# Conversion pieces, weight splits and second-layer weight sums placed anew over the blocks of the expert sweeps, and the last output tile stored in halves

## The chip, the cores and the metric

The kernel runs on one core of a Trainium2 chip. Five engines with instruction queues of their own work side by side: PE (TensorE, matmuls and their weight loads), DVE (VectorE), ACT (ScalarE), POOL (GpSimd) and SP (SyncE, which here only issues DMAs). The metric is the device time of one execution in microseconds (us), lower is better.

## The reference

Three layers follow each other on 2304 tokens of width 512 (4 batches of 576, 8 heads of 64):

```
scores = scale * q k^T;  ret = scores * Dmat (decay, lower triangle);  x = ret v
logits = x @ w_gate;  noisy = logits + log1p(exp(x @ w_noise)) * noise
top2 of 8 experts per token, softmax weights over the two
out[token] += weight * (relu(x @ w1[e]) @ w2[e])     # E=8, 512 -> 1024 -> 512
h = out @ w_in;  g = h * clip(h + 3, 0, 6) / 6;  y = g @ w_out   # 512 -> 2048 -> 512, w_in and w_out in float64
```

## The kernel before, in words

**Order of the work.** The program order of every engine is the order in which the code emits it: nothing is moved later. Each engine takes its instructions in that order, and SP takes its DMA issues in that order, so an instruction that waits holds up all that stand behind it on its engine.

**Precision.** Matmuls take a value as two parts, a rounded high part (written by ACT) and the remainder (written by DVE), and multiply three of the four pairs. So each weight has to be split: `w_load` (L557, L559) loads one quarter of an expert as two tiles of 512 KB, `w_split` (L567) sets up the four tiles for the parts, and `wstep` (L590 on ACT, L591 on DVE) does a quarter of that split at a time. Sixteen such steps belong to one expert.

**Sweeps and blocks.** `moe` (L778 on) goes through ten sweeps `si`. Sweep 0 takes the first 360 tokens of expert 0, sweep 1 its other 256; sweeps 2 to 7 take experts 1 to 6 with both runs of tokens together (360 and 256); sweeps 8 and 9 take expert 7 in two parts. Each sweep has eight blocks `f`, one for each 128 hidden units. In a block, PE first does the first product of each run (`g1`, L737, into the PSUM tiles `ga` and `gb`); ACT then writes the high part of the hidden values (L795), DVE the remainder (L796), and that frees the PSUM tile for the next first product into it. Then PE does the second product of the block before (`flush`, `g2`, L754). In sweep 1 a block has a single run, and `ga` and `gb` take turns.

**Work fitted between.** Beside this a block carries, in this order: up to two weight steps; one DMA load of a token tile for the next sweep (`x_load`, four issues at L682); one tile turned and split (`x_tile`: DVE transpose L690, ACT L692, and at the end of the block the DVE remainder L693); conversion pieces; and one step of `pr_step`.

**Conversion pieces.** The float64 weights of the last layer are turned into float32 in 64 pieces of 128 x 256: `cv_load` (SP, L614, 256 KB), `cv_abs` (ACT, L621), `cv_run` (DVE L632, L633, L635, L637; ACT L639; POOL L640, L641) and `cv_store` (SP, L648; the newest piece is always kept back). `CV` says how many pieces a block of sweeps 2 on runs: before, 2, 2, 2, 1, 1, 1, 1, 1. In a block of these sweeps the order is run, load, store, abs for each piece, so a piece is loaded ahead of its use. In sweep 1 before, blocks 5 to 7 load a piece each and block 7 does one abs.

**Sums.** `pr_step` (L1021 to L1031) makes sums and differences of the converted `w_in`, splits them and stores them to DRAM (`wc`), in seven jobs for each of eight column groups.

**The end.** `o_out` (L1221 on) copies the last four output tiles out of PSUM and stores them: the first three copies on ACT, the last on DVE; the first store from SP, the other three from ACT.

Of the kernel before, what the change touches and what calls it, by code (L numbers as in the profile page):

```python
# [12 lines left out]
AF = mybir.ActivationFunctionType  # L13
# [13 lines left out]
WN, WM = 2, 0  # L27
GA = 14
HS = np.array([0, 1, 3, 2, 4, 5, 7, 6])
CV = (2, 2, 2, 1, 1, 1, 1, 1)  # L30
MORE = -(-(N - CAP) // 128)
REG = CAP + 2048
assert MORE * 128 <= 2048
P = 128
# [44 lines left out]
class K:  # L79
# [686 lines left out]
    def moe(self, xs0):  # L766
        nc = self.nc
        xs = {(0, 0): xs0}
        self.prev = None
        for si, sw in enumerate(self.SW):  # L770
            nxt = self.SW[si + 1] if si + 1 < len(self.SW) else []
            todo = [(e, r, j) for e, r in nxt for j in range((3, 2)[r])]
            get = list(todo)
            e = sw[0][0]
            accs = None
            for f in range(8):
                n = e * 4 + f // 2
                cur = e * 4 if si in (0, len(self.SW) - 2) else n  # L778
                if f % 2 == 0:
                    if si == 0 or self.wsp <= cur + (4, 3, 3, 3, 3, 3, 3, 3, 5, 6)[si]:  # L780
                        self.w_split()
                if f % 2 == 0 and (si, f) != (0, 6) or (si, f) == (0, 7):
                    self.w_load()
                self.wstep(0, n)
                if (si, f) == (0, 7):
                    for s in todo:
                        self.x_fin(*s)
                tf = 3 if si == 1 or len(todo) > 3 else 4
                w, fi = self.w[n], f % 2
                subs = []  # L790
                for q, (_, r) in enumerate(sw):
                    c = (NA, NB)[r]
                    hh, hl = self.hid([P, c]), self.hid([P, c])
                    p = self.g1(self.parts(w, fi), xs[sw[q]], c, "ga" if (r == 0) == (f % 2 == 0 or len(sw) == 2) else "gb")
                    nc.scalar.activation(hh, p, AF.Relu)  # L795
                    nc.vector.scalar_tensor_tensor(hl, p, 0.0, hh.bitcast(F32), op0=OP.max, op1=OP.subtract)  # L796
                    subs.append((hh, hl, (RA, RB)[r]))
                if si == 0:
                    self.rstep()
                    self.send()  # L800
                    if f == 7:
                        for s in todo:
                            self.x_tile(s[0], xs[s[:2]], s[2], "acc", s[1])
                self.wstep()
                self.flush()
                later = []
                self.wstep(later=later if si == 1 else None)
                if accs is None:
                    accs = [[self.pacc([P, DM]) for _ in range(self.run_of(*s)[1])] for s in sw]
                self.prev = [(w, fi, [(*s, a) for s, a in zip(subs, accs)], f == 0, f == 7)]  # L810
                self.fin = (self.y_out, sw, accs)

                if si == 0:
                    for _ in range(3):
                        self.rstep()
                        self.send()
                    if f == 4:
                        while self.sent < NT or self.live:
                            self.rstep()
                            self.send()  # L820
                        self.count()
                        self.slots_in()
                g = 4 if si == 0 else 0
                if f == g:
                    for s in nxt:
                        if si == 0:
                            self.x_load(*s)
                        xs[s] = self.x_new(s[1])
                    if si < 2:
                        self.fill(range(2, E) if si else range(1, 2))  # L830
                if si and get:
                    ee, rr, j = get.pop(0)
                    self.x_load(ee, rr, [j])
                sub = None
                if si and f >= tf and todo:
                    ee, rr, j = todo.pop(0)
                    sub = self.x_tile(ee, xs[ee, rr], j, r=rr)
                if si > 1:
                    for _ in range(CV[f]):
                        self.cv_run()  # L840
                        self.cv_load()
                        self.cv_store()
                        self.cv_abs()
                elif si and f > 4:
                    self.cv_load()
                    if f == 7:
                        self.cv_abs()
                for s in later:
                    s()
                if sub:  # L850
                    sub()
                if (si > 2 or si == 2 and f > 3) and not (si in (6, 7) and f == 7):
                    self.pr_step()
                if si == 7 and f in (0, 2):
                    self.pr_step()
                if si == len(self.SW) - 1:
                    self.x2_prep(0, f - 1)
                    if f in (5, 7):
                        self.wc_load(f // 7)
            for s in sw:  # L860
                xs.pop(s)
# [358 lines left out]
    def o_out(self, t0, acc):  # L1220
        nc = self.nc  # L1221
        for j, a in enumerate(acc):
            o = self.row([P, DM])
            last = t0 + len(acc) == NT

            if last and j == len(acc) - 1:
                nc.vector.tensor_copy(o, a)
            else:
                nc.scalar.activation(o, a, AF.Copy)
            q = nc.scalar if last and j else nc.sync  # L1230
            q.dma_start(self.out[(t0 + j) * P:(t0 + j + 1) * P, :], o)


# [205 lines left out]
```

## Time and profile before

| | us |
|---|---|
| median of 3 runs | 935.1 (935.05 to 935.69) |
| the profiled execution, device time | 936.64 |
| its span, first to last instruction | 934.5 |
| PE busy in the span | 921.8 (99%) |
| DVE busy | 606.8 (65%) |
| ACT busy | 466.5 (50%) |
| POOL busy | 235.9 (25%) |

The device time of the profiled execution is 2.1 us over its span. Busy times of PE are modelled for pipelined matmuls. A timeline row gives the start, the time taken, the engine, the line, the operation, the tiles, and in square brackets how long the engine stood idle before it and for whom. PEld is PE's weight load, which runs ahead of the matmul that uses it. A row of an engine with "q" (SPq, ACTq) is a DMA issue.

### The profile page before, as it was taken

How to read it: one execution, taken by the hardware profiler on the slowest of the kernel's cores; microseconds unless marked ns; L12 is line 12 of the kernel's file. 1: busy time of each engine (PE TensorE's matmuls, PEld its weight loads, DVE VectorE, ACT ScalarE, POOL GpSimd, SP SyncE). 2: the span in 40 equal slices, each digit the busy share in tenths (PEclk: the TensorE clock that was granted, in tenths of full speed). 3: DMA queues.
4: the chain of work that ended last, by engine and by line, in shares of the span. 5: the costliest groups of instructions: out<-in, count | busy, mean ns of one | idle time of the engine just before them, and what ended most of it. 6: DMA issues, size and time to landing. Idle time of an engine off the chain costs nothing.

```text
span 934.5 us, 17789 instructions
## 1 busy us (share of the span) xinstructions
PE 921.8 (99%) x6314; PEld 818.2 (88%) x6314; DVE 606.8 (65%) x1327; ACT 466.5 (50%) x1025; POOL 235.9 (25%) x324
## 2 busy tenths in 40 slices
PE   9999999999999999999999999999999999999996
PEld 6887888988988889888888899999889998999985
DVE  5787747878879797787847446545745554564442
ACT  4666435455564645545544445544554464455432
POOL 1345531324233242432400221042004113300000
PEclk9999999999999999999999999999999999999999
DMA  9964877859879688896636787877578676846541
GB/s 339 386 243 147 304 243 232 238 187 280 259 241 282 227 256 271 248 267 218 224 111 214 265 298 252 307 247 240 188 262 270 205 258 227 271 166 228 167 150 49
DMA packets 123742, 221.22 MB, mean 237 GB/s; under 512 B 13037, under 2 KB 60915, under 8 KB 123643
## 3 DMA queue, kind: packets, MB, share of 16 engines
q1 hardware_dynamic: 113819, 190.47, 61.9%
q0 software_dynamic: 9392, 28.73, 9.1%
q8 instruction: 52, 0.85, 0.4%
q10 hardware_dynamic: 432, 0.79, 0.2%
q14 instruction: 47, 0.39, 0.1%
HBM read 163.97 MB, written 55.97 MB: 235 GB/s over the span
## 4 chain that ended last, share of the span: by engine, by line
PE 86%; DVE 7%; DMA 3%; issue 1%; ACT 1%; POOL 1%; SPq 0%; DVEq 0%; ACTq 0%; POOLq 0%
PE p L754 39%; PE ga L737 12%; PE gb L737 9%; PE mga L1168 7%; PE p L1168 5%; PE mgb L1168 2%; PE mtp L1168 2%; PE sc L225 2%; DVE b L591 1%; PE px L249 1%; PE p L293 1%; DVE cvt L635 1%; PE p L209 1%; DMA xe<-s,free 1%; DVE h L796 1%
## 5 line engine op out<-in xcount | busy, mean ns | idle before, releaser
L754 PE MATMUL p<-b,h 128*120 128x512 f32 (+1 forms) x1056 | 260.9, 395 | 0.0
L754 PEld LDWEIGHTS p<-b,h 128*120 128x120 f32 (+1 forms) x1056 | 189.2, 185 | 41.4 <-DVE h L796 0.4
L754 PE MATMUL p<-b,b 128*128 128x512 f32 x768 | 180.0, 390 | 0.0
L754 PEld LDWEIGHTS p<-b,b 128*128 128x128 f32 x768 | 142.3, 188 | 28.2
L737 PE MATMUL ga<-x,b 128*128 128x360 f32 (+1 forms) x768 | 134.4, 324 | 2.9 <-DVE h L796 2.9
L737 PEld LDWEIGHTS ga<-x,b 128*128 128x128 f32 x768 | 124.6, 188 | 12.1 <-DVE h L796 7.7
L640 POOL TENSOR_TENSOR cvl<-cvl,cvs 128x256 f32<-128x256 f32 x64 | 50.3, 785 | 229.9 <-ACT cva L621 163.0
L591 DVE TENSOR_TENSOR b<-b,b 128x512 fp32r<-128x512 f32 x128 | 89.6, 734 | 13.2 <-ACT b L590 12.9
L737 PE MATMUL gb<-b,b 128*128 128x256 f32 x672 | 89.7, 283 | 0.0
L737 PEld LDWEIGHTS gb<-b,b 128*128 128x128 f32 x672 | 86.9, 190 | 1.2
L885 POOL DMA_INDIRECT s<-yd,slotc x36 | 36.4, 1011 | 166.9 <-DVE x L991 48.4
L590 ACT ACTIVATE b<-b 128x512 fp32r<-128x512 f32 x128 | 74.1, 626 | 0.0
L1206 DVE SCALAR_TENSOR_TENSOR b<-s,b 128x512 fp32r<-128x512 f32 x64 | 44.3, 693 | 44.9 <-ACT b L1205 42.0
L1205 ACT ACTIVATE b<-s 128x512 fp32r<-128x512 f32 x64 | 40.5, 632 | 59.3 <-DVE s L1203 56.8
L796 DVE SCALAR_TENSOR_TENSOR h<-gb,h 128x256 fp32r<-128x256 f32 (+1 forms) x64 | 27.7, 433 | 50.2 <-PE p L754 35.2
L641 POOL TENSOR_TENSOR cvl<-cvt,cvl 128x256 f32<-128x256 f32 x64 | 58.2, 909 | 5.0
L1202 ACT ACTIVATE s<-s,three 128x512 f32<-128x512 f32 x64 | 45.9, 717 | 24.8 <-DVE s L1189 23.2
L1168 PE MATMUL mga<-b,b 128*128 128x256 f32 x384 | 56.3, 283 | 0.0
L1189 DVE TENSOR_TENSOR s<-p,mc 128x256 f32<-128x256 f32 x32 | 13.6, 424 | 65.4 <-PE p L1168 60.1
L1168 PEld LDWEIGHTS mga<-b,b 128*128 128x128 f32 x384 | 52.6, 191 | 2.5
L1203 DVE SCALAR_TENSOR_TENSOR s<-s,s 128x512 f32<-128x512 f32 x64 | 44.0, 687 | 7.5 <-DMA paced<-s 4.9
L1173 ACT ACTIVATE mc<-mga 128x256 f32<-128x256 f32 x64 | 24.6, 384 | 48.2 <-PE mga L1168 48.0
(206 smaller groups left out, 1433.6 us busy)
## 6 DMA issues: line engine op xcount, KB each, us to landing
b<-wc SPq DMA_DIRECT2D x112, 512.0 KB
b<-in_moe_w_dram SPq DMA_DIRECT2D x64, 512.0 KB
wc<-b SPq DMA_DIRECT2D x32, 512.0 KB
s<-xe SPq DMA_DIRECT2D x140, 64.0 KB
s<-in_moe_w_in_dram SPq DMA_DIRECT2D x32, 256.0 KB
s<-in_moe_w_out_dram SPq DMA_DIRECT2D x32, 256.0 KB
b<-wc SPq DMA_DIRECT2D x32, 256.0 KB
yd<-s SPq DMA_DIRECT2D x24, 240.0 KB
```

Of the source, the lines that this page charges most:

```text
L590: self.nc.scalar.activation(h, a, AF.Copy)
L591: rest = lambda h=h, l=l, a=a: self.nc.vector.tensor_sub(l, a, h.bitcast(F32))
L640: nc.gpsimd.tensor_mul(lf, lf, s.bitcast(F32))
L641: nc.gpsimd.tensor_add(lf, t.bitcast(F32), lf)
L737: nc.tensor.matmul(p, a[k], b[:, k, :n], start=(i == 0), stop=(i == 11))
L754: nc.tensor.matmul(a[:R], x[:, c], y[:, fi, :], start=(first and i == 0), stop=(last and i == 2))
L796: nc.vector.scalar_tensor_tensor(hl, p, 0.0, hh.bitcast(F32), op0=OP.max, op1=OP.subtract)
L1168: nc.tensor.matmul(t, w[:, u, k], x[:, z, k], start=(first and i == 0), stop=(last and i == 5), skip_group_check=True)
L1202: nc.scalar.activation(r, x, AF.Relu, bias=self.three)
L1203: v.scalar_tensor_tensor(x, r, 6.0, x, op0=OP.min, op1=OP.mult)
L1205: nc.scalar.activation(h[:, 0], x, AF.Copy, scale=1.0 / 6.0)
L1206: v.scalar_tensor_tensor(h[:, 1], x, 1.0 / 6.0, h[:, 0].bitcast(F32), op0=OP.mult, op1=OP.subtract)
```

## The change

- `CV` becomes 2, 2, 1, 1, 1, 1, 1, 1: ten pieces a sweep where there were eleven.
- In sweep 1, weight quarter 6 is split (and quarter 9 loaded) in blocks 2 and 3, where it was blocks 6 and 7.
- In sweep 1, blocks 2 to 7 each load a conversion piece (six), blocks 4 to 7 do one abs each, and blocks 5 to 7 run one piece each.
- In sweep 7, blocks 1 and 3 get a second step of the sums, and blocks 5 and 6 get none.
- The last output tile is copied in two halves of 256 columns, the left by ACT and stored from ACT, the right by DVE and stored from SP.

```diff
-CV = (2, 2, 2, 1, 1, 1, 1, 1)
+CV = (2, 2, 1, 1, 1, 1, 1, 1)
...
-                    if si == 0 or self.wsp <= cur + (4, 3, 3, 3, 3, 3, 3, 3, 5, 6)[si]:
+                    if si == 0 or self.wsp <= cur + (4, 5, 3, 3, 3, 3, 3, 3, 5, 6)[si] and (si, f // 4) != (1, 1):
                         self.w_split()
...
-                elif si and f > 4:
+                elif si and f > 1:
+                    if f > 4:
+                        self.cv_run()
                     self.cv_load()
-                    if f == 7:
+                    self.cv_store()
+                    if f > 3:
                         self.cv_abs()
...
-                if (si > 2 or si == 2 and f > 3) and not (si in (6, 7) and f == 7):
+                if (si > 2 or si == 2 and f > 3) and not (si == 6 and f == 7 or si == 7 and f > 4):
                     self.pr_step()
-                if si == 7 and f in (0, 2):
+                if si == 7 and f < 4:
                     self.pr_step()
...
-
+            q = nc.scalar if last and j else nc.sync
             if last and j == len(acc) - 1:
-                nc.vector.tensor_copy(o, a)
-            else:
-                nc.scalar.activation(o, a, AF.Copy)
-            q = nc.scalar if last and j else nc.sync
+                for k, eng in enumerate((nc.scalar.copy, nc.vector.tensor_copy)):
+                    s = slice(k * 256, k * 256 + 256)
+                    eng(o[:, s], a[:, s])
+                    (nc.scalar, nc.sync)[k].dma_start(self.out[(t0 + j) * P:(t0 + j + 1) * P, s], o[:, s])
+                continue
+            nc.scalar.activation(o, a, AF.Copy)
             q.dma_start(self.out[(t0 + j) * P:(t0 + j + 1) * P, :], o)
```

## Rows read from the trace of the kernel before

**Rows 1.** The page: busy by engine, then the chain that ended last, by engine.
```profile
PE 921.8 (99%) x6314; PEld 818.2 (88%) x6314; DVE 606.8 (65%) x1327; ACT 466.5 (50%) x1025; POOL 235.9 (25%) x324
...
PE 86%; DVE 7%; DMA 3%; issue 1%; ACT 1%; POOL 1%; SPq 0%; DVEq 0%; ACTq 0%; POOLq 0%
```

**Rows 2.** Waits of weight loads, 95 to 560: us in total, times, longest.
```profile
PEld ga L737 <- DVE h L796: 7.7, 14, 1.2
```

**Rows 3.** Timeline of PEld, holes in sweeps 5 and 7.
```profile
343.63 1.47 PEld L737 LDWEIGHTS ga<-x,b 128*128 128x128 f32 x9 [0.72 <-DVE h L796]
...
449.03 1.94 PEld L737 LDWEIGHTS ga<-x,b 128*128 128x128 f32 x12 [0.27 <-DVE h L796]
...
456.57 1.45 PEld L737 LDWEIGHTS ga<-x,b 128*128 128x128 f32 x9 [0.82 <-DVE h L796]
```

**Rows 4.** Waits of SP's queue: us in total, times, longest.
```profile
SPq L682 <- DMA xe<-s,free: 5.3, 1, 5.3
```

**Rows 5.** Timeline of SP's issues, sweep 1.
```profile
137.75 9.37 SPq L682 DMA_DIRECT2D s<-xe  x20
...
148.16 0.47 SPq L559 DMA_DIRECT2D b<-in_moe_w_dram  x1
```

**Rows 6.** Timeline of DVE, sweep 1.
```profile
141.19 0.73 DVE L690 STREAM_TRANSPOSE xp<-s 128x512 f32<-128x512 f32 x1 [2.63 <-DMA s<-xe]
...
145.57 0.41 DVE L796 SCALAR_TENSOR_TENSOR h<-ga,h 128x256 fp32r<-128x256 f32 x1
145.90 0.72 DVE L690 STREAM_TRANSPOSE xp<-s 128x512 f32<-128x512 f32 x1
...
148.65 0.72 DVE L690 STREAM_TRANSPOSE xp<-s 128x512 f32<-128x512 f32 x1
...
150.03 0.69 DVE L693 TENSOR_TENSOR b<-xp,b 128x512 fp32r<-128x512 f32 x1
150.64 0.41 DVE L796 SCALAR_TENSOR_TENSOR h<-ga,h 128x256 fp32r<-128x256 f32 x1
```

**Rows 7.** Timeline of ACT, sweep 1.
```profile
144.33 0.60 ACT L692 ACTIVATE x<-xp 128x512 fp32r<-128x512 f32 x1 [1.45 <-DVE xp L690]
144.83 0.38 ACT L795 ACTIVATE h<-ga 128x256 fp32r<-128x256 f32 x1
```

**Rows 8.** Timeline of PE, end of sweep 1 and start of sweep 2.
```profile
146.18 1.55 PE L754 MATMUL p<-b,h 128*128 128x512 f32 x6
...
151.11 2.25 PE L737 MATMUL ga<-x,b 128*128 128x360 f32 x12 [0.54 <-DVE h L796]
```

**Rows 9.** DMA by stretch: length, busy of PE, PEld, DVE, ACT, POOL, PEclk, DMA share, GB/s.
```profile
169.50:173.50 4.00, 4.00 (x29) 3.87 (x28) 3.64 (x9) 1.24 (x4) 1.79 (x3) 1.00 1.02 317
...
184.00:186.00 2.00, 2.00 (x15) 2.00 (x14) 1.77 (x6) 1.44 (x4) 0.00 (x0) 1.00 1.08 258
```

**Rows 10.** Two conversion loads issued by SP, and ACT's wait for the first.
```profile
160.06 0.90 SPq L614 DMA_DIRECT2D s<-in_moe_w_in_dram  x2
...
163.55 0.44 ACT L621 ACTIVATE cva<-s 128x256 f32<-128x256 f32 x1 [2.01 <-DMA s<-in_moe_w_in_dram]
```

**Rows 11.** Timeline of DVE: first operations of two conversion pieces, and what follows them.
```profile
158.00 0.29 DVE L632 TENSOR_SCALAR cva<-cva 128x256 f32<-128x256 f32 x1
...
159.32 0.29 DVE L632 TENSOR_SCALAR cva<-cva 128x256 f32<-128x256 f32 x1
...
161.71 0.52 DVE L796 SCALAR_TENSOR_TENSOR h<-ga,h 128x360 fp32r<-128x360 f32 x1
```

**Rows 12.** The end: timeline of ACT and DVE, and the last stretch (columns as Rows 9).
```profile
927.14 0.60 ACT L1229 ACTIVATE s<-p 128x512 f32<-128x512 f32 x1 [0.46 <-PE p L754]
927.44 0.69 DVE L1227 COPY s<-p 128x512 f32<-128x512 f32 x1 [6.09 <-PE p L754]
927.77 2.01 ACTq L1231 DMA_DIRECT2D out_dram<-s  x2
...
931.00:934.50 3.50, 0.00 (x0) 0.00 (x0) 0.00 (x0) 0.00 (x0) 0.00 (x0) 0.50 0.05 16
```

## Prediction made before the change was run

> **What bounds the kernel now.** I read the page first, then the chain, the waits of PE's weight loads, and then the timelines of the places where those waits lie. PE is busy for 921.8 of 934.5 us and carries 86% of the chain [rows 1]. There is therefore little to win: only holes in PE's stream count. In the stretch of the sweeps nearly all of these have one cause: the first product of a block waits until DVE has written the hidden remainder (L796) and so freed its PSUM tile. They come to 7.7 us in 14 places [rows 2]. DVE takes its work in order, so L796 is late where the DVE work of the block before it (weight steps, token tile, conversion pieces, sums) was long. The question for each part of the change is whether it shortens DVE's queue at such a hole, and whether it makes some engine wait in front of an L796 where none waited.
>
> **Eleven pieces become ten in each of sweeps 2 to 7.** The piece goes from block 2. Its DVE work stands behind the L796 of block 2 and ahead of that of block 3, so only a hole at the start of block 4 or later can shrink. One conversion piece costs DVE 1.32 us alone (158.00 to 159.32), and 2.39 us when POOL works on the piece before it (159.32 to 161.71) [rows 11]. Block 4 of sweep 5 has such a hole, 0.72 us as the weight loads show it [rows 3]; with 1.3 us or more less ahead of it, it goes. PE drains its queue for part of it, so I take 0.55, with bounds of 0.3 and 0.72. The holes at blocks 2 and 3 of the other sweeps stand ahead of the removed piece and stay. The pieces taken out return as three in sweep 1 and three in blocks 6 and 7 of sweep 7 and block 0 of sweep 8; these last stand where no hole is, and 1.32 us of DVE work is hidden there by one block of PE work. Without that cover they would cost up to 1.3 us each.
>
> **Sums in sweep 7.** Block 1 gets one more job (a split), and block 2 has one conversion piece less. The hole at block 3 (0.27 us) grows, the one at block 4 (0.82 us) closes [rows 3]. Both lie on one saturated stretch of DVE, so what one loses the other mostly wins; I take 0, with bounds of -0.8 and +0.8. The DMA issues of these jobs move one or two blocks ahead in SP's queue; what stands behind them are token tiles and pieces needed a block or more later, which covers them.
>
> **The weight split in sweep 1.** Four steps move from blocks 6 and 7 to blocks 2 and 3, where DVE and ACT have idle time. This alone would take 2.7 us of DVE work (four L591 at 0.67 us, an estimate from the L693 beside them, 0.69 us [rows 6]) out of a crowded stretch. But the split of quarter 6 brings the load of quarter 9 with it, two DMAs of 512 KB, and those now stand in SP's queue between the token tiles 1 and 2 of expert 1.
>
> **The order of SP's queue in sweep 1 decides.** SP cannot load the tokens of expert 1 until the fill of the token buffer has landed [rows 4]; its first issue comes at 137.75, and 20 issues take 9.37 us, 0.47 each [rows 5]. Nothing in the change makes this earlier. Two tiles of four issues are out at 137.75 + 8 x 0.47 = 141.5. Then come, new, the two weight loads (0.47 each [rows 5]) until 142.4, tile 2 until 144.3, and the first conversion load at 144.3 to 144.7; after it tile 3, a conversion load, tile 4, and so on. Before, the first conversion load stood behind all 20 issues.
>
> **Where the wait appears.** In the change block 4 ends with `cv_abs` for that first piece, on ACT, and behind it in ACT's queue stands the high part of the hidden values (L795) of block 5, on which the second product of block 5 hangs. Before, ACT finished the tile work of block 4 at 144.33 + 0.60 = 144.93, and L795 of block 5 ran at 144.83 [rows 7]. Now ACT must stand until the piece has landed. When is that? By bytes: behind 141.5 there are 512 + 512 + 256 + 256 KB, 1.57 MB. In a stretch with weights, tokens and pieces in the same order the engines moved 317 GB/s at full share, in a busier one 258 [rows 9]: 5.0 or 6.1 us. From the end of an issue to use it takes 1.6 us (tile 0: out at 139.6, DVE starts at 141.19 [rows 6]). That gives 148.1 or 149.2. Another row gives a lower end: a conversion load issued at 160.06 let ACT go at 163.55, 3.5 us later [rows 10], so 144.3 + 3.5 = 147.8. I take 148.2, nearest to the stretch with the same mix.
>
> **The chain from there.** `cv_abs` takes 0.44 [rows 10], L795 0.38 [rows 7]: the hidden values of block 5 are there at 149.0, and L796 follows at about 149.05, instead of 145.57 [rows 6]. PE would have started that second product at 146.18 [rows 8], so it stands for 2.8 us. After that DVE is the bound. From one L796 to the next it now does: L796 0.33 (145.57 to 145.90), transpose 0.72, a conversion piece 1.32 [rows 11], the tile's remainder 0.61 (150.03 to 150.64) [rows 6], 2.98 us in all. So L796 of block 6 comes at 152.0 and that of block 7 at 155.0, where it was at 150.64 [rows 6]. It is this one that lets the first product of sweep 2 start [rows 8]. Sweep 2 starts 155.0 - 150.64 = 4.4 us later. Nothing gives that back: PE is full from there on, and DVE and PE are late by the same amount. Bounds: 4.0 with the piece landing at 147.8; 5.4 with 149.2, and 1.07 us more in each of two rounds if POOL's work beside them stretches a piece as in [rows 11], 7.5 together. I add nothing for POOL, because a single piece has left DVE before POOL starts on it.
>
> The conversion stores of blocks 6 and 7 make SP wait for POOL, some 3 us after DVE has run a piece. Behind them stand a weight quarter and the tokens of the next expert, used more than 15 us later; that covers it.
>
> **The last tile in halves.** DVE's copy of 0.69 us halves, and SP can issue the right half while ACT is still at work. ACT has its third copy at 927.14 and two issues in 2.01 us after 927.77 [rows 12]; now a half copy (some 0.38 us, as the 256-column L795 [rows 7]) stands between these two issues. So the left half is issued no earlier than the whole tile was, and SP, which had been free, now carries a store. I take -0.1, with bounds of -0.5 and +0.4.
> The Trainium skill ("DMA: Bandwidth & Descriptors", section "Anatomy of one DMA — SWDGE (gpsimd) path") gives a transfer a fixed part of about 2.0 us and a part by bytes, fitted for POOL's queue. By that, half a tile would land 0.3 us sooner, an estimate from that page; no row here times an output store alone, and the sum would be 0.2 us lower.
>
> **The sum.** +4.4 - 0.55 + 0 - 0.1 = +3.75 us. On the profiled execution that is 936.64 + 3.75 = 940.4; it is 1.5 us slower than the median of the runs, so on the median it is 935.1 + 3.75 = 938.9.
>
> **Rivals.**
> 1. The forecast: ACT and DVE wait in sweep 1 for loads that SP issues too late. Speaking for it: every step is an order of queues that the rows show. Speaking against it: no row shows an abs waiting this long. 938.9, from 937.0 to 943.0 with the bounds. Chance 0.68.
> 2. Not slower: the conversion load is there in time. Its place is block 4 of sweep 1. If the piece lands before 144.9, ACT loses nothing, and if tile 2 lands by 145.9 DVE goes on as before [rows 6, 7]. Then L796 of block 7 comes at 145.57 + 2 x 2.98 = 151.5, 0.9 us late only, and the total is 935.1 + 0.9 - 0.55 - 0.1 = 935.4. This needs SP to start 3.3 us earlier, or the pieces to overtake the weights. Chance 0.18.
> 3. The clock falls in the new hole. At the end of the kernel the granted clock is 0.50 (1.2 GHz) from 931.00 on, with PE idle since about 927.4 [rows 12], and 1.00 in the stretches of the sweeps shown [rows 9]; the new hole of 2.8 us is of a like length. At half the clock the next second product, first product and second product (about 1.4 us each, by the pitch 146.18 to 151.11 for three of them less the hole [rows 8]) take 4.2 us more, of which the wait until 155.4 hides 2.1. That gives 941.0. Chance 0.08.
> The Trainium skill ("TensorE: Matmul & The Clock Gate", section "HAM oscillation — how this bites in real kernels") tells of a loop whose matmuls wait for a DMA between tiles and start each tile at the lower clock. By that rule this rival would be the forecast; the trace agrees at the kernel's end, and shows no hole of this length between matmuls.
> 4. Faster: rival 2, and the DVE time freed in block 2 also closes the holes ahead of it. If 5 of the 7.7 us [rows 2] went, it would be 935.4 - 5 = 930. It speaks against this that the blocks after 4 have no holes, so nothing is carried from one sweep to the next. Chance 0.06.
>
> **How the numbers follow.** The time is that of rival 1, 938.9. The range runs from 935.3, which takes in about half of rival 2, to 943.0, the forecast with its upper bounds (7.5 + 0.8 + 0.4 - 0.3 = 8.4, of which not all come together). About 0.2% (1.9 us) is what a measurement of this kernel can tell from no change. Slower than 937.0 are rivals 1 and 3: 0.76; within it rival 2: 0.18; faster rival 4: 0.06.
>
> **What would show it.** In the changed profile, `cva` on ACT in sweep 1 should wait for a DMA for about 3 us, with L795 of block 5 right behind it; PE's second product of block 5 should start near 149.0 and sweep 2 near 155.5. SP should issue two weight tiles after its eighth token issue. The hole in block 4 of sweep 5 should be gone, those in blocks 2 and 3 of the other sweeps still there. I am wrong if the first abs does not wait, if SP's queue starts its tokens well before 137.75, or if holes past sweep 1 shrink by more than 1 us in sum.

## The result, and the profile after

The changed kernel takes 943.55 us (median of 6 runs, 943.09 to 944.40) where the kernel before takes 935.39 beside it: a ratio of 1.0088, with a 95% interval of 1.0075 to 1.0101. So it is 8.2 us slower; 3.8 were forecast. The profiled execution took 943.69 us, with a span of 941.6.

Busy time by engine from the page of the changed kernel (before: [rows 1]):

```profile
PE 923.0 (98%) x6314; PEld 818.9 (87%) x6314; DVE 603.1 (64%) x1327; ACT 467.6 (50%) x1026; POOL 236.2 (25%) x324
```

PE has the same number of matmuls and 1.2 us more of busy time; the span has grown by 7.1. The rest is new holes. The waits of PE's weight loads (us in total, times, longest) name the two engines that are late (before: [rows 2]):

```profile
PEld ga L737 <- DVE h L796: 7.3, 10, 1.9
PEld p L754 <- ACT h L795: 4.5, 3, 3.5
```

The second row is new: second products that wait for ACT. To see where the time went, I cut each span at the first L795 of every sweep in ACT's timeline (for sweep 2 of the changed kernel it starts at 157.51). Stage lengths in us, from one such row to the next; "end" runs from the start of the last matmul to the end of the span:

| stage | before | after | difference | forecast |
|---|---|---|---|---|
| until the first L795 | 97.34 | 96.05 | -1.29 | none |
| sweep 1 | 24.92 | 30.26 | +5.34 | +4.4 |
| sweep 5 | 56.06 | 55.48 | -0.58 | -0.55 |
| sweep 6 | 55.63 | 55.24 | -0.39 | 0 |
| sweep 7 | 56.26 | 57.21 | +0.95 | 0 |
| sweep 8 | 26.27 | 28.49 | +2.22 | 0 |
| end | 7.49 | 8.35 | +0.86 | -0.1 |
| the other stages together | 610.54 | 610.48 | -0.06 | 0 |

I take the first line as no effect of the change: over all the kernels below, whose code there is the same, it lies between 95.7 and 97.9. Without it the differences sum to 8.34; the medians differ by 8.16.

**Sweep 1.** The timelines of SP, ACT, DVE and PE in the changed kernel (before: [rows 5 to 8]; subtract 1.29 from a time of before to compare):

```profile
136.92 3.66 SPq L682 DMA_DIRECT2D s<-xe  x8
140.67 0.39 SPq L557 DMA_DIRECT2D b<-in_moe_w_dram  x1
141.16 0.45 SPq L559 DMA_DIRECT2D b<-in_moe_w_dram  x1
141.66 1.88 SPq L682 DMA_DIRECT2D s<-xe  x4
143.65 0.36 SPq L614 DMA_DIRECT2D s<-in_moe_w_in_dram  x1
```

```profile
148.11 0.43 ACT L621 ACTIVATE cva<-s 128x256 f32<-128x256 f32 x1 [3.99 <-DMA s<-in_moe_w_in_dram]
148.45 0.36 ACT L795 ACTIVATE h<-ga 128x256 fp32r<-128x256 f32 x1
```

```profile
148.85 0.42 DVE L796 SCALAR_TENSOR_TENSOR h<-ga,h 128x256 fp32r<-128x256 f32 x1 [4.00 <-ACT h L795]
...
151.62 0.41 DVE L796 SCALAR_TENSOR_TENSOR h<-gb,h 128x256 fp32r<-128x256 f32 x1
...
154.75 0.41 DVE L796 SCALAR_TENSOR_TENSOR h<-ga,h 128x256 fp32r<-128x256 f32 x1
```

```profile
148.87 2.27 PE L754 MATMUL p<-b,h 128*128 128x512 f32 x6 [3.33 <-ACT h L795]
150.93 2.57 PE L737 MATMUL ga<-b,b 128*128 128x256 f32 x12
...
155.22 2.25 PE L737 MATMUL ga<-x,b 128*128 128x360 f32 x12 [0.34 <-DVE h L796]
```

This is the forecast's chain, link by link: the two weight loads behind the eighth token issue, the abs that waits 3.99 us, L795 right behind it, PE's hole, and then DVE rounds of 2.77 and 3.13 us up to the first product of sweep 2. PE's 2.27 and 2.57 us, against 1.55 [rows 8] and 1.60 for the like products before, tell of the clock. The windows of the changed kernel (columns as in [rows 9]) show it:

```profile
149.70:153.11 3.41, 3.41 (x15) 3.12 (x14) 3.27 (x10) 1.79 (x5) 1.46 (x2) 0.50 0.75 245
153.20:170.00 16.80, 16.46 (x99) 14.86 (x98) 13.81 (x32) 9.96 (x25) 6.23 (x8) 1.00 0.73 223
```

The granted clock was at its lower level (0.50, 1.2 GHz) for 3.41 us behind the hole, and 1.00 after.

**Sweep 7.** PE's timeline before, with a hole ahead of block 2 (the matmuls of block 4, whose weight load is in [rows 3], have one of 0.38 us), then in the changed kernel:

```profile
442.03 2.24 PE L737 MATMUL ga<-x,b 128*128 128x360 f32 x12 [0.53 <-DVE h L796]
```

```profile
445.49 2.25 PE L737 MATMUL ga<-x,b 128*128 128x360 f32 x12 [0.89 <-DVE h L796]
453.64 2.25 PE L737 MATMUL ga<-x,b 128*128 128x360 f32 x12 [0.96 <-DVE h L796]
```

The hole ahead of block 4 has closed, the one ahead of block 3 has grown to 0.96, and the one ahead of block 2 is 0.89.

**Sweep 8.** SP's issues; SP's wait for POOL from 484 to 520 (us in total, times, longest); then ACT and PE:

```profile
494.40 2.03 SPq L682 DMA_DIRECT2D s<-xe  x4
496.53 2.27 SPq L648 DMA_DIRECT2D wout<-cvl  x2
498.89 3.18 SPq L682 DMA_DIRECT2D s<-xe  x4
502.18 1.05 SPq L567 DMA_DIRECT2D s<-wout  x2
```

```profile
SPq L648 <- POOL cvl L641: 7.3, 2, 5.9
```

```profile
504.95 0.63 ACT L590 ACTIVATE b<-s 128x512 fp32r<-128x512 f32 x1 [0.79 <-DMA s<-wout]
...
509.38 0.38 ACT L795 ACTIVATE h<-ga 128x256 fp32r<-128x256 f32 x1
```

```profile
509.81 1.98 PE L754 MATMUL p<-b,h 128*128 128x512 f32 x6 [0.49 <-ACT h L795]
...
516.03 2.24 PE L737 MATMUL ga<-x,b 128*128 128x360 f32 x12 [1.42 <-DVE h L796]
```

The last two conversion stores (L648) wait for POOL in SP's queue. Behind them stand a token tile of sweep 9 and the loads of the converted output weights (L567 is that load in the trace); ACT then waits for those weights, and L795 behind it is late. Before, the last pieces are done in sweep 7 and PE's only hole of note here is this one:

```profile
509.77 2.25 PE L737 MATMUL ga<-x,b 128*128 128x360 f32 x12 [0.74 <-DVE h L796]
```

**The end.** ACT and DVE (before: [rows 12]):

```profile
934.34 0.37 ACT L1232 COPY s<-p 128x256 f32<-128x256 f32 x1 [0.41 <-ACT s L1235]
...
934.75 0.42 DVE L1232 COPY s<-p 128x256 f32<-128x256 f32 x1 [7.20 <-ACT s L1232]
```

The two halves do not run side by side: DVE's begins when ACT's has ended.

### The profile page after: what moved, and what is told of

Read it like the earlier page. It is cut to its first block, busy times and chain, and to the rows that moved or that the text cites. A ratio compares the mean times of both kernels' runs of the same rounds, so it can differ in the third digit from the quotient of the medians.

```text
span 941.6 us, 17798 instructions
## 1 busy us (share of the span) xinstructions
PE 923.0 (98%) x6314; PEld 818.9 (87%) x6314; DVE 603.1 (64%) x1327; ACT 467.6 (50%) x1026; POOL 236.2 (25%) x324
## 4 chain that ended last, share of the span: by engine, by line
PE 88%; DVE 5%; DMA 3%; issue 1%; SPq 1%; ACT 1%; POOL 1%; ACTq 0%; DVEq 0%
PE p L754 40%; PE ga L737 12%; PE gb L737 9%; PE mga L1171 7%; PE p L1171 5%; PE mgb L1171 2%; PE mtp L1171 2%; PE sc L225 2%; DMA s<-xe 1%; PE px L249 1%; DVE b L591 1%; PE p L293 1%; PE p L209 1%; DMA xe<-s,free 1%; PE p L281 1%
## 5 line engine op out<-in xcount | busy, mean ns | idle before, releaser
L796 DVE SCALAR_TENSOR_TENSOR h<-gb,h 128x256 fp32r<-128x256 f32 (+1 forms) x64 | 27.8, 435 | 60.7 <-PE p L754 48.5
L795 ACT ACTIVATE h<-gb 128x256 fp32r<-128x256 f32 (+1 forms) x64 | 25.2, 394 | 52.0 <-PE gb L737 52.0
```

## The experiments

The theory was that of the prediction for sweep 1, and for the stages that it had at nothing the readings above. Medians stand beside the kernel before on the same chip.

**1. The weight split alone.** The kernel before with the condition of the split from the diff.

> The kernel before with one part of the change alone: in sweep 1 weight quarter 6 is split in blocks 2 and 3, and with it quarter 9 is loaded there. Theory Q (order of SP's queue): the 1 MB of quarter 9 stands ahead of token tile 2, which DVE turns near 147 instead of 145.9; two rounds later sweep 2 starts 0 to 1.5 us later than before, so 935.4 to 937. Theory L (DVE load alone): four weight steps, 2.7 us of DVE work, leave the crowded end of sweep 1 and the hole of about 1 us ahead of sweep 2 goes: 934.4.

Measured: 937.15, ratio 1.0012 (1.0003 to 1.0020). Without any new conversion work the early split makes the kernel slower, by slightly more than theory Q had. DVE waits for token tile 2; then PE:

```profile
147.60 0.73 DVE L690 STREAM_TRANSPOSE xp<-s 128x512 f32<-128x512 f32 x1 [3.14 <-DMA s<-xe]
...
149.20 1.87 PE L754 MATMUL p<-b,h 128*128 128x512 f32 x6 [1.57 <-ACT h L795]
...
152.26 2.24 PE L737 MATMUL ga<-x,b 128*128 128x360 f32 x12 [1.19 <-DVE h L796]
```

**2. The split without the load that comes with it.** As 1, but blocks 2 and 4 of sweep 1 load no weights, so that quarter 9 comes as late as before:

```diff
-                if f % 2 == 0 and (si, f) != (0, 6) or (si, f) == (0, 7):
+                if (f % 2 == 0 and (si, f) not in ((0, 6), (1, 2), (1, 4))) or (si, f) == (0, 7):
                     self.w_load()
```

> As the run with the split alone, but quarter 9 is loaded in block 6 of sweep 1, where it was before. Theory Q: tile 2 is no longer late, DVE has less to do, the hole ahead of sweep 2 goes: 934.4, and 1 us or more below the run with the load. Theory L: the same time as the run with the load, since DVE's work is the same.

Measured: 934.85, ratio 0.9991 (0.9982 to 1.0000). Both holes of experiment 1 are gone. So the price of the split is its load's place in SP's queue, 2.3 us between the two medians; without it this kernel is the only one that came out below the kernel before, by no more than the measurement can tell, and its sweep 1 of 24.56 us is no shorter than that of some kernels with the code of before there (24.54 to 25.19).

**3. The conversion pieces of sweep 1 alone.** The kernel before with the changed branch of sweep 1 (loads from block 2, abs from block 4, runs from block 5), splits and loads as before.

> The kernel before with the conversion in sweep 1 alone (six loads, four abs, three pieces run there; eleven pieces a sweep after it). Theory Q: the first piece's load stands behind token tile 2 but not behind quarter 9, lands near 146.8, and ACT and L795 of block 5 wait for it: PE has a hole of 1.5 us there, and sweep 2 starts 3 to 4.5 us later, 938.5 to 940, with no hole added in sweep 8. Theory L: three pieces of 1.32 us on DVE make sweep 2 about 2 us late, with no wait of ACT for a DMA: 937.5.

Measured: 940.38, ratio 1.0050 (1.0038 to 1.0062), 0.4 us over theory Q's range. The wait that theory Q told of is there: ACT's first abs waits 1.79 us for its load. PE's timeline:

```profile
146.25 1.66 PE L754 MATMUL p<-b,h 128*128 128x512 f32 x6 [1.14 <-ACT h L795]
...
154.43 3.27 PE L737 MATMUL ga<-x,b 128*128 128x360 f32 x12 [3.45 <-DVE h L796]
```

The pieces alone cost as much as the whole change does in sweep 1, because the weight steps are still in blocks 6 and 7 beside them: the hole moves to the start of sweep 2. There the clock fell too, from about 155 to 159, and this time PE had nothing to wait for: the first product took 3.27 us instead of 2.25, the next one 2.13 instead of 1.60.

**4. The abs moved behind the wait.** The changed kernel with the abs of sweep 1 just ahead of the piece that needs it:

```diff
                     if f > 4:
+                        self.cv_abs()
                         self.cv_run()
                     self.cv_load()
                     self.cv_store()
-                    if f > 3:
+                    if f == 7:
                         self.cv_abs()
```

> The changed kernel, with ACT's abs of sweep 1 moved: it stands just ahead of the piece that needs it (blocks 5 to 7) instead of at the end of the block before, so that L795 of block 5 no longer stands behind an abs that waits for its load. Theory A (DVE's chain from the late token tile is the bound as well): the 3.3 us hole ahead of the second product of block 5 goes, but the holes behind it grow, because DVE still waits for token tile 2 at about 147.5 and then goes round in 3 us a block; sweep 2 starts 0.3 to 1 us earlier than in the changed kernel, 942.6 to 943.3. Theory B (the wait of ACT is the whole price of sweep 1): sweep 2 starts about 3 us earlier, 940.5. If the clock falls only behind a hole of 3 us, it stays at 1.00 here.

Measured: 946.41, ratio 1.0114 (1.0098 to 1.0129); both theories had it faster. ACT, DVE and PE:

```profile
144.62 0.38 ACT L795 ACTIVATE h<-ga 128x256 fp32r<-128x256 f32 x1
148.94 0.52 ACT L692 ACTIVATE x<-xp 128x416 fp32r<-128x416 f32 x1 [3.94 <-DVE xp L690]
...
148.18 0.73 DVE L690 STREAM_TRANSPOSE xp<-s 128x512 f32<-128x512 f32 x1 [2.40 <-DMA s<-xe]
149.80 0.29 DVE L632 TENSOR_SCALAR cva<-cva 128x256 f32<-128x256 f32 x1 [0.90 <-ACT cva L621]
...
156.18 3.97 PE L737 MATMUL ga<-x,b 128*128 128x360 f32 x12 [2.89 <-DVE h L796]
```

Two things come out. L795 of block 5 now runs at 144.62, and the hole of 3.33 us is gone. But DVE can turn token tile 2 only at 148.18, when it has landed; ACT stands until then, and L795 of block 6 behind it is late (149.99), so PE stands for 1.44, 0.95 and 2.89 us after all. That is theory A's cause: the token tile behind the weight load is a bound beside the first abs. And the edit puts a wait of its own into DVE: each piece now waits 0.9 to 1.0 us for its abs, which stands on ACT behind the token tile, so a round takes 4.1 us instead of 3.0. The clock fell ahead of sweep 2 and stayed low for 6.8 us, with PE as the bound. This tells why the abs stood a block ahead; it does not price the wait on its own.

**5. The last piece a block earlier.** The changed kernel with two pieces in block 7 of sweep 7 and none in sweep 8:

```diff
-                    for _ in range(CV[f]):
+                    for _ in range(CV[f] + (si == 7 and f == 7)):
```

> The changed kernel, with the 64th conversion piece run in block 7 of sweep 7 (two pieces there), so that block 0 of sweep 8 has none. Theory S (the piece in sweep 8 costs by what stands behind it: DVE's L796 of block 1, and SP's last stores, which wait for POOL ahead of the token tiles and the weights of sweep 9): the holes at about 509 and 514 to 516 go back to the one of 1.0 us that the kernel before has there, -1.5 to -2.3 us: 941.2 to 942. Rival (the holes of sweep 8 come from the shorter CV in blocks 2 of the sweeps, that is from the order of the loads and not from this piece): 943.5, holes unchanged.

Measured: 946.98, ratio 1.0126 (1.0111 to 1.0142): 3.4 us slower than the changed kernel, where 1.5 to 2.3 faster was expected. SP, ACT and PE:

```profile
485.03 9.91 SPq L648 DMA_DIRECT2D wout<-cvl  x3
...
507.60 0.63 ACT L590 ACTIVATE b<-s 128x512 fp32r<-128x512 f32 x1 [3.69 <-DMA s<-wout]
...
512.72 2.40 PE L754 MATMUL p<-b,h 128*128 128x512 f32 x6 [3.65 <-ACT h L795]
```

All of the last stores now stand ahead of everything else that sweep 8 issues, and the wait for POOL moves the output weights further back: ACT waits for them until 507.60 instead of 504.95. So the piece on DVE is not the larger cost; SP's order is.

**6. The last stores later.** The changed kernel with its piece in place, but the two stores issued in block 4 of sweep 8:

```diff
                         self.cv_load()
-                        self.cv_store()
+                        if si != 8 or f > 3:
+                            self.cv_store()
                         self.cv_abs()
```

> The changed kernel, with the 64th piece where it is (block 0 of sweep 8), but the two last conversion stores issued in block 4 of sweep 8 instead of block 0, so that SP no longer waits for POOL ahead of the token tiles of sweep 9. If SP's wait makes the late holes of sweep 8 (509 and 514 to 516), they shrink by 1.3 to 1.8 us and the 0.54 us hole at 497.6 stays: 941.7 to 942.3. If DVE's piece alone makes them, nothing changes: 943.5.

Measured: 942.29, ratio 1.0077 (1.0064 to 1.0091), 1.3 us below the changed kernel. SP and PE:

```profile
494.15 4.08 SPq L682 DMA_DIRECT2D s<-xe  x8
498.33 0.86 SPq L567 DMA_DIRECT2D s<-wout  x2
...
514.01 2.25 PE L737 MATMUL ga<-x,b 128*128 128x360 f32 x12 [0.74 <-DVE h L796]
```

The weights go out 3.6 us earlier in the sweep (3.85 by the spans, 0.25 of which this run was ahead), ACT's waits for them are gone, and sweep 8 takes 26.73 us (28.49 in the changed kernel, 26.27 before). So of the 2.22 us, 1.76 are SP's wait for POOL and 0.46 is what is left, which no run prices on its own. These sizes are rough: with the stores early, sweep 8 takes 27.76 (experiment 9), 28.49 and 29.29 us (experiment 4); with the stores late, 26.73 and 26.72 (experiment 8).

**7. The end alone, and with two tiles.** The kernel before with the halves of the diff; then the same with an SBUF tile for each half:

```diff
                     s = slice(k * 256, k * 256 + 256)
+                    o = self.row([P, DM])
                     eng(o[:, s], a[:, s])
```

> The kernel before with the last output tile in halves alone. Theory W (a wait between the halves): DVE's half copy starts only when ACT's has ended, SP's store and with it SP's way through the branch at the end come later, and the time from the last matmul to the end grows from 7.1 to about 8.0 us: 936.3. Rival: the halves run side by side, and the end takes 7.1 us or less: 935.2.

> The kernel before with the last output tile copied in halves by ACT and DVE, each half into an SBUF tile of its own. If DVE waited for ACT because both write one SBUF tile, the two halves now run side by side, and the tail behind the last matmul is 7.0 to 7.4 us: 935.2 to 935.8 where the kernel before has 935.4. If they wait for each other because both read one PSUM tile, DVE's half still starts after ACT's and the tail stays at about 8.1 us: 936.3 to 937.

Measured: 937.11, ratio 1.0016 (1.0007 to 1.0025), and 936.75, ratio 1.0011 (1.0002 to 1.0021). With two tiles the wait stays:

```profile
928.64 0.37 ACT L1230 COPY s<-p 128x256 f32<-128x256 f32 x1 [0.41 <-PEq L1279]
...
929.05 0.42 DVE L1230 COPY s<-p 128x256 f32<-128x256 f32 x1 [7.20 <-ACT s L1230]
```

So the tile that is written does not make it; what the two still share is the PSUM tile that they read. Before, ACT and DVE copied at the same time, but out of two tiles [rows 12]. The wait in the trace is one on a semaphore that ACT's copy raises. The Trainium skill ("PSUM — Partial Sum Buffer", section "Terms") has a rule that would ask for such a wait: two engines must not touch one bank at once, two reads among them. No run here let them, and none gave each half a PSUM tile of its own.

**8. Three causes out at once.** The changed kernel with the load of experiment 2, the stores of experiment 6 and the end as before.

> The changed kernel with three causes taken out at once: the load of weight quarter 9 issued behind the token tiles of sweep 1 as in the kernel before (the split stays early), the last conversion stores in block 4 of sweep 8, and the last output tile copied whole as before. If the three prices add up, it is the changed kernel's 943.5 less 1.6 (sweep 1: the first conversion load goes out 0.95 us earlier and has 1 MB less ahead of it, so the piece is there at about 146.7, L795 of block 5 runs at 147.5 and two rounds of 2.98 us end at 153.5), less 1.3 (sweep 8), less 0.9 to 1.3 (tail): 939.3 to 939.8. What is left over the kernel before is then the three conversion pieces in sweep 1 and the holes of sweep 7. If the clock falls behind a late uncovered hole, 941 to 941.5. If the causes hide each other, the sum is smaller: 941 to 942.

Measured: 939.57, ratio 1.0050 (1.0035 to 1.0064), inside the expected 939.3 to 939.8. That is in part luck, for the parts are not those of the forecast. In the profiled execution (939.02) sweep 1 gave back 3.07 us where 1.6 was expected, sweep 8 1.77 and the end 1.39, together 6.2, while the stage until the first L795, whose code is the same, took 1.87 more (97.92). Each of the three causes is thus seen in its own stage; that their prices add up is not shown by the median. PE's timeline at the start of sweep 2; the clock stayed at 1.00:

```profile
154.03 2.25 PE L737 MATMUL ga<-x,b 128*128 128x360 f32 x12 [1.87 <-DVE h L796]
```

**9. The sums as before.** The changed kernel with both conditions of `pr_step` from the kernel before.

> The changed kernel with the jobs of the moe2 sums spread over sweep 7 as in the kernel before (blocks 0 and 2 get two jobs, block 7 none). The two holes of sweep 7 (0.89 at 445.5 and 0.96 at 453.6) are 0.75 us more than before. If the sums make that, it goes: 942.6 to 943.0. If it comes from the pieces (the shorter block 2 shifts DVE's stretch, and blocks 6 and 7 now have pieces), the time stays at 943.5 and the holes with it.

Measured: 942.48, ratio 1.0082 (1.0068 to 1.0096), 1.1 us below the changed kernel. Sweep 7 takes 56.03 us instead of 57.21, and only one hole of 0.3 us or more stands there, the one ahead of block 2:

```profile
445.67 2.25 PE L737 MATMUL ga<-x,b 128*128 128x360 f32 x12 [0.89 <-DVE h L796]
```

**10. Another spread.** An attempt at a faster kernel: the kernel before with the pieces and sums placed otherwise; and the same on top of experiment 2.

```diff
-CV = (2, 2, 2, 1, 1, 1, 1, 1)
+CV = (1, 1, 2, 1, 2, 1, 2, 1)
...
-                if si == 7 and f in (0, 2):
+                if si == 7 and f in (4, 6):
```

> The kernel before with its eleven pieces a sweep placed otherwise: one each in blocks 0, 1, 3, 5, 7 and two each in blocks 2, 4, 6 (before: two each in 0, 1 and 2), and the two extra sums of sweep 7 in blocks 4 and 6 instead of 0 and 2. If the holes of sweeps 2 to 7 come from DVE's load in the blocks just ahead, they shrink, by 1 to 3 us in sum: 932.5 to 934.5. If block 2's pair alone makes them (its place is kept), 935.4.

> The kernel before with the weight split of quarter 6 moved early in sweep 1 without its load (that part alone gave 934.85), and the pieces placed as in the run with pieces in blocks 2, 4 and 6. If the two gains add up: 0.6 to 1 us below that run, 931.5 to 934. If the pieces bring nothing, 934.85.

Measured: 939.40, ratio 1.0049 (1.0034 to 1.0063), and 938.77, ratio 1.0036 (1.0022 to 1.0050): both slower than the kernel before, where both were expected faster. The waits of PE's weight loads in the first of them:

```profile
PEld ga L737 <- DVE h L796: 5.6, 7, 1.3
PEld gb L737 <- ACT b L692: 3.8, 5, 0.9
...
PEld gb L737 <- DVE b L693: 1.9, 5, 0.4
```

The old holes shrink by 2.1 us as expected, but now PE waits for the tokens of the next sweep (L692 and L693 into `b`), 5.7 us in all, at five of the sweeps' starts. With two pieces in block 6, DVE turns the last token tile later in block 7: in sweep 2 at 205.47 instead of 204.45, where the sweep itself had begun 0.55 earlier. With the pairs in blocks 0 to 2 this wait does not arise.

## Why the prediction was right in part, and where it failed

Four terms carry the miss. The cover that was to hide the moved piece in sweep 8, the end taken at -0.1 and the sums in sweep 7 taken at 0 failed as steps; in sweep 1 the step was right and the landing of the first piece mis-sized.

**Sweep 1: the mechanism was right, the size 0.9 too small.** In the times of before, SP issued the first conversion load at 144.94, forecast 144.3, for the greater part because its token issues began 0.46 later than in [rows 5] when both are counted from the first L795 of the kernel. The load was in use 4.46 us after its issue; the forecast had 3.9. Together that is 1.2 us, and PE's second product of block 5 started 1.16 us late (150.16, forecast 149.0). The two DVE rounds took 5.90 us, forecast 5.96. So the term that was mis-sized is the landing, 148.2 for a measured 149.4, half of it through the later issue; the figure by 258 GB/s (149.2) was the better one.

**What causes the price** is less one-sided than the prediction said. The lengths of sweep 1, in us:

| | no conversion pieces | with the pieces |
|---|---|---|
| split late, as before | 24.92 | 30.33 (experiment 3) |
| split early, load late | 24.56 (experiment 2) | 27.19 (experiment 8) |
| split and load early | 27.41 (experiment 1) | 30.26 (the change) |

With the split early, the load costs 2.9 or 3.1 and the pieces 2.6 or 2.9: two prices of a size, which add here. The prediction gave all to one chain. The early split itself is worth 3.1 us once the pieces are there (30.33 to 27.19), and the load that it brings takes that back. Kernels with the same code in sweep 1 differ by up to 0.8 there: 24.54 to 25.19 with the code of before (four), 30.02 to 30.81 with that of the change (four), so no difference below that size counts.

**Rival 3 came true, and cost nothing.** The clock fell behind the hole of 3.33 us. The Trainium skill ("TensorE: Matmul & The Clock Gate", section "HAM oscillation — how this bites in real kernels"), cited beside that rival, tells of a loop whose matmuls start at the lower clock behind a wait for a DMA; the trace agrees but for the start, since PE ran 0.83 us at 1.00 before the clock fell. But the price forecast for it, 2.1 us, did not come: the slow products ended at 153.50, and DVE's L796 of block 7 came at 154.75 from DVE's own queue. Here DVE was the bound for longer than the clock was low, and so the low clock was hidden. In experiments 3 and 4 it fell where PE was the bound, and there the first product of sweep 2 took 1.0 and 1.7 us longer.

**Sweep 5** lost its hole, -0.58 for -0.55, and most of that is luck. Experiments 1 to 3, which keep eleven pieces, have no hole between matmuls there either, and 55.67 to 55.71 us, so only some 0.2 is left for the piece taken out. What they lack is a pause of DVE just ahead of one L637, which the kernel before has in sweep 5 and, 0.47 us long, in sweep 6 at 384.32:

```profile
332.85 0.29 DVE L637 TENSOR_SCALAR cvs<-cvt 128x256 int32<-128x256 int32 x1 [0.46 <-DVE cvt L635]
```

The 0.39 us of sweep 6 go with that second pause: experiments 1 to 3 have 55.25 to 55.29 there without it. What DVE waits for in the pause is open; the operation that the row names is the one just before it.

**Sweep 7: 0 was wrong by 0.95**, just outside the bounds of 0.8. The step "what one loses the other mostly wins" failed: the hole ahead of block 4 closed (0.38), but the one ahead of block 3, behind the job added in block 1, reached 0.96. Experiment 9 puts this one down to the sums, as it is gone there. The hole ahead of block 2 (0.53 to 0.89) is not theirs: experiment 9 keeps it at 0.89, and experiment 8, with the sums of the change, has 0.53. It comes with the same pause of DVE; the changed kernel has it in this sweep, experiment 8 does not:

```profile
443.48 0.29 DVE L637 TENSOR_SCALAR cvs<-cvt 128x256 int32<-128x256 int32 x1 [0.46 <-DVE cvt L635]
```

```profile
443.97 2.24 PE L737 MATMUL ga<-x,b 128*128 128x360 f32 x12 [0.53 <-DVE h L796]
```

So of the 0.95, about 0.36 is the pause. The prediction put the holes of sweeps 5 and 7 down to the amount of DVE work alone; the pause of sweep 5 stands in the trace that it was read from.

**Sweep 8: "hidden" failed, by 2.2 us.** The prediction counted the moved piece as 1.32 us of DVE work and let its store be: the stores' wait for POOL was looked at in sweep 1 only, where what stands behind is used late. In sweep 8 loads stand behind it that are used within 3 us of their issue. This is the largest miss, and it was an instruction of a moved step that had not been followed into its queue.

**The end: -0.1 became +0.86**, outside the bounds. The prediction followed ACT's issues and took for granted that two engines can copy halves of one tile side by side. Over the runs here the stage takes 6.87 to 7.64 us with a whole copy (seven kernels) and 8.09 to 8.35 with halves (seven kernels).

The errors of these terms, 0.94 - 0.03 - 0.39 + 0.95 + 2.22 + 0.96, give 4.65 in the profiled executions. The medians moved 8.16 where 3.75 was forecast, 4.41 more; that 4.65 is also the distance from 938.9 to 943.55 is chance, since the kernel before was 0.29 slower beside the change than in the forecast.

## What to carry to other kernels

Follow each instruction of a moved step into its own queue, in every place where the step lands: here the costliest ones were a weight load and two stores on SP, an engine that does no arithmetic. An issue that must wait for its producer belongs behind the loads that are needed soon. Before a copy is cut in two for two engines, see whether both halves lie in one PSUM tile.

## What the runs showed of the hardware

- Behind PE's holes of 3.20 us (experiment 6), 3.33 (the change), 3.45 (experiment 3) and 3.65 (experiment 5, sweep 8) the granted clock went from 1.00 to 0.50. It did so within the holes of 3.85 us (experiment 5, sweep 1), 3.77 (experiment 9) and 2.89 (experiment 4, which has two smaller ones just ahead). Behind the 1.87 us hole of experiment 8 it stayed at 1.00. It was low for 6.8 us in experiments 4 and 9 and for 3.4 us in each of the others.
- A 256 KB load that SP issued at 143.65, behind two of 512 KB, was in use at 148.11, 4.46 us later. With only token tiles ahead (experiment 8) the same load, issued at 143.79, was in use at 146.93, after 3.14 us.
- In eight of the fourteen traces DVE pauses for 0.46 or 0.47 us just ahead of one L637, in sweeps 5 and 6 (the kernel before and experiment 7) or in sweep 7 (the change and experiments 4, 5, 6 and 9). What it waits for is open.
